# A Fourier mixing kernel: both turns of a batch in four chunks, the inverse matrices formed on the chip

## The chip, the cores and the metric

The kernel runs on one core of a Trainium2 chip. The metric is device time in microseconds. The kernel before was run three times: 861.09 us in the median, 858.69 to 861.26. Engines are named as in the profile: PE (TensorE matmuls), PEld (its weight loads), DVE (VectorE), ACT (ScalarE), POOL (GpSimd), SP (SyncE); SP, POOL and, in one place, ACT issue DMAs from their instruction queues.

## What is computed

The input x has 8 batches of 3008 tokens with 256 channels. First comes a global filter along the sequence, then a two-layer network with a leaky activation whose slope belongs to the hidden unit:

```python
X = np.fft.rfft(x, axis=1)
Y = X * (filt_r + 1j * filt_i)[None]
x = np.fft.irfft(Y, n=3008, axis=1).reshape(24064, 256)
h = x @ w_in                                    # 256 -> 2048
g = np.maximum(h, 0) + alpha * np.minimum(h, 0)
out = g @ w_out                                 # 2048 -> 256
```

Inputs and output are float32; the kernel works in float16 with float32 accumulation.

## The kernel before

**The transform.** 3008 is 47 times 64, so a token index is written as 64 times s1 plus s2, and the transform is done in two steps, forward and back. For each batch there are four kinds of pieces:

- piece_a (L162, 16 per batch): the transform over s1. The input chunk `xs` has 94 partitions (two halves of s2, each with the 47 values of s1), and each matmul with `wf1_s` gives 96 rows and 512 columns, evicted into `asb`. Input comes in four chunks of two DMAs each (load_x, L120, on POOL's queue, which turns float32 into float16).
- piece_b (L184, 12 per batch): the transform over s2 with its twiddle factors, one 128 x 128 matrix `twf_s[:, k1]` per frequency k1, two frequencies per piece. It reads `at`. DVE then multiplies the result with the filter into `uu` and with the filter's swapped halves `filts_s` into `ww`. Batch 0 uses piece_b0 (L195), which gets the swapped product from two more matmuls of 64 columns of weights, so that it need not wait for `filts_s`.
- piece_c (L211, 12 per batch): the inverse over s2, `twi_s[:, k1, 0]` times `uu` plus `twi_s[:, k1, 1]` times `ww`, evicted into `v`.
- piece_d (L238, 16 per batch): the inverse over s1 with `wi3_s`; its weights are slices of `zt`, so that its result comes transposed, channels on partitions, as the network wants it; evicted into `yT`.

**The turns.** Between piece_a and piece_b, rows and partitions change places (s1's frequency must leave the partitions, s2 must come in), and again between piece_c and piece_d. Both turns go through DRAM. On the way in, save_a (L171) writes a quarter of `asb` at a time to `a_dram[b, row, s, d]` in runs of 4 KB, and turn_a (L175) then reads the whole batch with four DMAs in runs of 512 bytes (one channel row): 3072 runs. In batch 0 it is eight half DMAs, half from SP's queue and half from ACT's. On the way back, turn_c (L224) writes a quarter of `v` with four DMAs in runs of 512 bytes, and after the last quarter reads everything in four DMAs in runs of 4 KB, each of which brings what four pieces of piece_d need. Every tile named here exists once; `a_dram` and `v_dram` have room for all batches.

**The network.** Tokens go in blocks of 512 (one of 384 per pair of batches), 48 blocks. A block has 16 steps. In step j, Block.up (L327) makes the 128 hidden rows j with two matmuls into `hps`; every second step ACT evicts two of them into `gt`, and DVE applies the slope with three instructions. In the same step Block.down (L344) does a sixteenth of the previous block's second layer, four matmuls of 256 columns; finished results go through `osb` to DRAM with stores on SP's queue (L316).

**The order of work** is written out by hand; no scheduler moves anything. Up to piece_d number 3 of batch 0 there is a prologue (L258 to L297) without network work. Then the main loop (L392) counts steps through all blocks, 768 in all, and after up and down of a step it issues the pieces that `plan` holds for that step. plan_fft (L364) puts a batch's pieces there: piece_a from step a0 every ga steps, a save after every fourth, the load of the next batch's chunk one step later, turn_a at step ta, piece_b from b0 every gap steps, piece_c three steps after its piece_b, turn_c, and piece_d from d0. Since every engine and every DMA queue works in program order, a DMA on SP that waits holds back all DMAs behind it, stores too.

Two PSUM banks (`psF`) are handed out in turn to piece_a, piece_b, piece_c and piece_d, so a piece waits until the one two before it has been read by ACT or DVE. `p_uw` holds two pairs of `uu` and `ww`, `p_x` four input chunks.

**Loads in the prologue.** SP loads `wf1_s`, the slopes, and half of `twf_s`; after turn_a the two halves of `twi_s` (L265, L267), the second half of `twf_s` and `wi3_s`. POOL loads the input of batch 0, then all eight parts of the filter (L142), and copies one column of `at` into a tile `gate` (L273), which makes its queue wait for the turn; then come `win_s` and `wout_s` (L275, L277), a copy from `zt` (L293), and the input of batch 1 (L295). `filts_s` is copied from `filt_s` on SP behind turn_c (L291).

Of the kernel before, what the change touches and what calls it, by code (L numbers as in the profile page):

```python
# [13 lines left out]
NFFT = 3008  # L14
# [11 lines left out]
def _build_consts():  # L26

    s1 = np.arange(N1)
    s2 = np.arange(N2)
    k1 = np.arange(NK1)
    p = np.arange(64)
    k2 = np.where(p < 32, p, 95 - p)
    g = np.where(p < 32, 1.0, -1.0)

    a1 = 2 * np.pi * np.outer(s1, k1) / N1
    wf1 = np.zeros((2 * N1, 96))  # L40
    wi3 = np.zeros((96, 2 * N1))
    scale = np.where(k1 == 0, 1.0, 2.0) / NFFT
    for h in range(2):
        r = slice(h * N1, h * N1 + N1)
        wf1[r, h * 48 : h * 48 + NK1] = np.cos(a1)
        wf1[r, h * 48 + NK1 : h * 48 + 48] = -np.sin(a1)
        wi3[h * 48 : h * 48 + NK1, r] = (np.cos(a1) * scale).T
        wi3[h * 48 + NK1 : h * 48 + 48, r] = (-np.sin(a1) * scale).T
# [4 lines left out]
    twf = np.empty((128, NK1, 128))  # L53
    twf[:64, :, :64], twf[64:, :, :64] = c, s
    twf[:64, :, 64:], twf[64:, :, 64:] = -s * g, c * g
    ec, es = c.transpose(2, 1, 0), s.transpose(2, 1, 0)
    gp = g[:, None, None]
    twi = np.empty((128, NK1, 2, 128))
    twi[:64, :, 0, :64], twi[:64, :, 0, 64:] = ec, es
    twi[64:, :, 0] = -twi[:64, :, 0]  # L60
    twi[:64, :, 1, :64], twi[:64, :, 1, 64:] = -es * gp, ec * gp
    twi[64:, :, 1] = twi[:64, :, 1]
    return wf1, wi3, twf, twi
# [3 lines left out]
def kernel(  # L67
# [11 lines left out]
    wf1_np, wi3_np, twf_np, twi_np = _build_consts()  # L79
# [3 lines left out]
    twi_d = nc.inline_tensor(twi_np.astype(np.float16), name="c_twi")  # L83
# [12 lines left out]
    a_dram = dram.tile([NB, 96, NH, D], FP16, name="a_dram")  # L96
    v_dram = dram.tile([NB, 96, NH, D], FP16, name="v_dram")
# [6 lines left out]
    twi_s = konst.tile([128, NK1, 2, 128], FP16, name="twi_s")  # L104
    filt_s = konst.tile([128, NK1, D], FP16, name="filt_s")
# [32 lines left out]
    xc = {(0, c): load_x(0, c) for c in range(4)}  # L138
    nc.sync.dma_start(out=al16, in_=moe_alpha.rearrange("(j p) -> j p", p=128))
    nc.sync.dma_start(out=twf_s[:, 0:12], in_=twf_d.ap()[:, 0:12])  # L140
    for ka, kb in ((0, 12), (12, 24)):
        load_filt(filt_s, 0, filt_r, ka, kb)  # L142
        load_filt(filt_s, 64, filt_i, ka, kb)
# [8 lines left out]
    class Fft:  # L152
# [18 lines left out]
        def save_a(self, c):  # L171
            s = slice(8 * c, 8 * c + 8)
            nc.sync.dma_start(out=a_dram[self.b, :, s], in_=self.asb[:, s])

        def turn_a(self, eng, ka=0, kb=NK1):  # L175
            for h in range(2):
                for c in range(2):
                    r = h * 48 + c * NK1
                    q = c * 64 + NH * h
                    eng.dma_start(  # L180
                        out=self.at[q : q + NH, ka:kb],
                        in_=a_dram[self.b, r + ka : r + kb].rearrange("k s d -> s k d"))
# [40 lines left out]

        def turn_c(self, q):  # L224
            k = 6 * q
            for h in range(2):
                for c in range(2):
                    r = h * 48 + c * NK1 + k
                    p = c * 64 + NH * h
                    nc.sync.dma_start(  # L230
                        out=v_dram[self.b, r : r + 6].rearrange("k s d -> s k d"),
                        in_=self.v[p : p + NH, k : k + 6])
            if q == 3:
                for g in range(4):
                    s = slice(8 * g, 8 * g + 8)
                    nc.sync.dma_start(out=self.zt[:, s], in_=v_dram[self.b, :, s])
# [20 lines left out]

    f0 = Fft(0)  # L258
    for i in range(16):
# [33 lines left out]
    nc.gpsimd.tensor_copy(gate[0:96, 1:2], f0.zt[:, 31, 0:1])  # L293
    for c in range(4):
# [69 lines left out]
    def plan_fft(b, a0, ga, ta, b0, gap, d0):  # L364
# [3 lines left out]
        for c in range(4):  # L368
            put(a0 + ga * (4 * c + 3), f.save_a, c)
            if b + 1 < NB:  # L370
                put(a0 + ga * (4 * c + 3) + 1,
                    lambda b=b, c=c: xc.update({(b + 1, c): load_x(b + 1, c)}))
        put(ta, f.turn_a, nc.sync)
# [61 lines left out]
```

## Time and profile before

| what | us |
|---|---|
| median of three runs | 861.09 |
| profiled execution, span from first to last instruction | 861.4 |
| PE busy | 799.4 |
| DVE busy | 612.9 |
| ACT busy | 586.6 |
| first matmul of piece_a (L168) | 7.54 |
| first matmul of piece_b0 (L200) | 33.05 |
| last matmul of piece_c of batch 0 (L221) | 53.81 |
| first matmul of piece_d (L243) | 63.08 |
| first matmul of the main loop (L332) | 64.62 |
| first matmul of piece_b of batch 1 (L188) | 110.36 |

The profiled execution spans 861.4 us, 0.3 above the median of the runs. How to read it: a line of the profile gives a line of the kernel, the engine, the operation, and output and input tile by name; "idle before" is the time in which the engine stood still just before, with what released it. PE's busy time is modelled from pipelined matmuls, so 93% does not say how near PE is to its peak; distances from start to start tell more. "PEclk" is the share of TensorE's clock that was granted; the clock fell to half after longer idle stretches of PE and came back some microseconds after work began again. The share of the DMA engines is a mean over 16. In the window 20 to 40 us that share reads 1.14, that is, all 16 were full.

### The profile page before, as it was taken

Reading aid. Unit: us, or ns where it says so; the run is one execution under the profiler, and the core shown is the slowest. Engines: PE = TensorE matmul, PEld = TensorE weight load, DVE = VectorE, ACT = ScalarE, POOL = GpSimd, SP = SyncE. Lnnn points to the kernel's source line nnn. Section 1 sums busy time; section 2 is a strip of 40 time slices with the busy share of each in tenths; the row PEclk is TensorE's granted clock in tenths of the full one; section 3 lists DMA queues with packets and bytes.
Section 4 is the critical chain, followed back from the end, with each engine's and each line's share of the span. In section 5 each row is a group of like instructions: output and inputs, shape, how many; then the busy total and the mean of one; then the engine's idle time right before and its main releaser. Section 6 shows DMA issues by size and latency. Waiting matters only on the chain.

```text
span 861.4 us, 15404 instructions
## 1 busy us (share of the span) xinstructions
PE 799.4 (93%) x5809; PEld 541.7 (63%) x5809; DVE 612.9 (71%) x1361; ACT 586.6 (68%) x817; POOL 41.4 (5%) x85
## 2 busy tenths in 40 slices
PE   3458989979999999999999999999999999999997
PEld 1134556756666766676666766676666766676665
DVE  2246668758877787678877787778877788777773
ACT  2027757767787767777777767777777866677663
POOL 4103000000000000000000000000000000000000
PEclk9989989999999999999999999999999999999999
DMA  9989835761368224772268323682148122411111
GB/s 212 250 171 197 179 69 133 157 144 41 75 148 199 60 62 97 172 158 51 53 162 195 73 64 83 164 181 50 43 120 186 50 68 50 129 38 39 39 41 49
DMA packets 95378, 95.95 MB, mean 111 GB/s; under 512 B 8312, under 2 KB 85128, under 8 KB 95176
## 3 DMA queue, kind: packets, MB, share of 16 engines
q1 hardware_dynamic: 85448, 78.19, 35.8%
q0 software_dynamic: 8256, 16.00, 12.3%
q10 hardware_dynamic: 1600, 0.79, 0.5%
q8 instruction: 45, 0.74, 0.4%
q14 instruction: 29, 0.24, 0.1%
HBM read 59.55 MB, written 49.81 MB: 127 GB/s over the span
## 4 chain that ended last, share of the span: by engine, by line
PE 70%; DVE 13%; ACT 7%; DMA 6%; issue 2%; SPq 1%; POOL 0%; ACTq 0%; DVEq 0%; POOLq 0%
PE hps L332 29%; PE op L350 28%; ACT gt L337 6%; DVE gt L341 4%; DVE m L340 4%; PE psF L168 3%; DVE ww L192 3%; DVE uu L191 3%; PE psF L221 2%; DMA at<-a_dram 2%; PE psF L243 2%; DMA a_dram<-asb 2%; PE psF L220 1%; DMA xs<-in_x_dram 1%; PE psF L188 1%
## 5 line engine op out<-in xcount | busy, mean ns | idle before, releaser
L337 ACT ACTIVATE gt<-hps 128x1024 f16<-128x1024 f32 (+1 forms) x384 | 385.1, 1003 | 134.6 <-PE hps L332 134.1
L332 PE MATMUL hps<-yT,win_s 128*128 128x512 f16 (+1 forms) x1536 | 454.3, 377 | 1.1 <-ACT yT L250 1.0
L350 PE MATMUL op<-wout_s,gt 128*128 128x256 f16 x3008 | 453.3, 273 | 0.6 <-DVE gt L341 0.6
L350 PEld LDWEIGHTS <-gt 128*128 128x128 f16 x3008 | 294.4, 98 | 192.5 <-issue 2.8
L340 DVE TENSOR_SCALAR m<-gt,alm_s 128x512 f16<-128x512 f16 (+1 forms) x768 | 233.5, 346 | 164.1 <-ACT gt L337 162.8
L341 DVE TENSOR_TENSOR gt<-gt,m 128x1024 f16<-128x1024 f16 (+1 forms) x384 | 261.6, 681 | 24.3 <-DVE m L340 0.9
L332 PEld LDWEIGHTS <-win_s 128*128 128x128 f16 x1536 | 145.6, 98 | 31.6 <-issue 5.0
L250 ACT ACTIVATE asb<-psF 96x512 f16<-96x512 f32 x120 | 70.7, 593 | 40.2 <-PE psF L168 40.2
L250 ACT ACTIVATE v<-psF 128x512 f16<-128x512 f32 x84 | 50.2, 598 | 34.9 <-PE psF L221 34.9
L250 ACT ACTIVATE yT<-psF 128x376 f16<-128x376 f32 x120 | 58.1, 484 | 20.9 <-PE psF L243 20.7
L191 DVE TENSOR_TENSOR uu<-psF,filt_s 128x512 f16<-128x512 f32 x84 | 57.4, 683 | 6.7 <-PE psF L188 6.7
L355 ACT ACTIVATE osb<-op 128x512 f32<-128x512 f32 x96 | 56.3, 587 | 6.9 <-PE op L350 3.7
L168 PE MATMUL psF<-xs,wf_s 94*96 94x512 f16 x120 | 47.8, 398 | 11.0 <-DMA xs<-in_x_dram 8.3
L192 DVE TENSOR_TENSOR ww<-psF,filts_s 128x512 f16<-128x512 f32 x84 | 57.1, 679 | 0.0
L123 POOL DMA_DIRECT2D xs<-in_x_dram x64 | 32.9, 522 | 458.2 <-PE psF L168 457.1
L243 PE MATMUL psF<-wi_s,zt 96*128 96x94 f16 x504 | 42.7, 207 | 10.8 <-DMA zt<-v_dram 9.0
L243 PEld LDWEIGHTS <-zt 96*128 96x128 f16 x512 | 36.3, 100 | 18.9 <-DMA zt<-v_dram 9.3
L221 PE MATMUL psF<-ww,twi_s 128*128 128x256 f16 x168 | 41.1, 272 | 6.2 <-DVE ww L192 3.5
L220 PE MATMUL psF<-uu,twi_s 128*128 128x256 f16 x168 | 42.9, 272 | 1.1 <-ACT yT L250 0.5
L188 PE MATMUL psF<-at,twf_s 128*128 128x256 f16 x168 | 32.3, 274 | 8.1 <-issue 4.5
L220 PEld LDWEIGHTS <-twi_s 128*128 128x128 f16 x192 | 19.0, 99 | 18.0 <-issue 13.2
L250 ACT ACTIVATE v<-op 128x512 f16<-128x512 f32 x12 | 7.2, 597 | 32.4 <-PE op L221 32.4
(35 smaller groups left out, 130.8 us busy)
## 6 DMA issues: line engine op xcount, KB each, us to landing
out_dram<-osb SPq DMA_DIRECT2D x128, 128.0 KB
a_dram<-asb SPq DMA_DIRECT2D x32, 384.0 KB
v_dram<-v SPq DMA_DIRECT2D x128, 96.0 KB
zt<-v_dram SPq DMA_DIRECT2D x32, 384.0 KB
xs<-in_x_dram POOLq DMA_DIRECT2D x64, 188.0 KB, 5.1
at<-a_dram SPq DMA_DIRECT2D x28, 384.0 KB
twi_s<-c_twi SPq DMA_DIRECT2D x2, 768.0 KB
filts_s<-filt_s SPq DMA_DIRECT2D x2, 768.0 KB
```

What stands on the lines that cost most here:

```text
L168: nc.tensor.matmul(ps[0:96], wf1_s, xs[:, o : o + 512], start=True, stop=True)
L191: nc.vector.tensor_mul(uu, px, filt_s[:, 2 * kp : 2 * kp + 2])
L192: nc.vector.tensor_mul(ww, px, filts_s[:, 2 * kp : 2 * kp + 2])
L220: nc.tensor.matmul(pv[:, kh], twi_s[:, k1, 0], uu[:, kh], start=True, stop=False)
L221: nc.tensor.matmul(pv[:, kh], twi_s[:, k1, 1], ww[:, kh], start=False, stop=True)
L243: nc.tensor.matmul(ps[:, m], self.zt[:, 8 * g + 4 * mh + m, dh * 128 : dh * 128 + 128], wi3_s, start=True, stop=True)
L250: nc.scalar.activation(o, i, AF.Copy)
L332: nc.tensor.matmul(self.hps[:, j % 2, 0:tn], win_s[:, kt, j * 128 : (j + 1) * 128], yT[:, kt, self.t0 : self.t0 + tn], start=(kt == 0), st ...
L337: nc.scalar.activation(g[:, :, 0:tn], self.hps[:, :, 0:tn], AF.Copy)
L340: nc.vector.tensor_scalar(m[:, i, 0:tn], g[:, i, 0:tn], 0.0, a, OP.min, OP.mult)
L341: nc.vector.tensor_add(g[:, :, 0:tn], g[:, :, 0:tn], m[:, :, 0:tn])
L350: nc.tensor.matmul(self.op[:, si % 2], self.gts[k][:, 128 * si : 128 * si + 128], wout_s[:, k], start=(k == 0), stop=(k == 15))
```

## The change

It has four parts.

1. **The turns run in four chunks, scattered when written and contiguous when read.** `a_dram` becomes `[batch, 4, 8, 96, 256]`: save_a of a quarter c writes 96 x 8 runs of 512 bytes, and the new turn_a(c) reads that quarter into 32 partitions of `at`, 12 KB contiguous for each. `v_dram` becomes `[batch, 4, 12, 64, 256]`: save_c(q) writes a quarter with two DMAs of 64 partitions (runs of 512 bytes as before), and turn_c(q) reads it into 24 partitions of `zt`, 16 KB contiguous each. All turns are issued by SP. Partition order in `at` and rows in `asb` and `zt` change with it, and so do the constants `wf1_s`, `wi3_s` and `twf_s`.
2. **`twi_s` is formed on TensorE.** It is no longer a constant of 1.5 MB. form_twi transposes 64 columns of `twf_s` at a time by a matmul with a permutation matrix or its negative (`perm_s`, 64 KB): eight matmuls of 128 columns, one eviction of 512 columns, for two frequencies. Six of the twelve go ahead of batch 0's piece_a, six after it. Both halves of `twf_s` are loaded at the start for that.
3. **Loads are held.** The second half of the filter is loaded behind the first gate (`at` of batch 0 has landed), with `win_s`; `wout_s` is loaded behind the second gate (`zt` has landed), ahead of batch 1's input.
4. **The plan moves.** piece_c comes four steps after its piece_b. Batch 1: turns from step 17 on, piece_b from step 34 every 4 steps (it was 40, every 3). Batch 2: turns from step 80 (it was 86). Later batches: turns from 33 steps before the reference step (it was 22). save_c comes five steps after a quarter's last piece_b, its turn four steps later.

```diff
-    twi_d = nc.inline_tensor(twi_np.astype(np.float16), name="c_twi")
+    perm_d = nc.inline_tensor(perm_np.astype(np.float16), name="c_perm")
...
-    a_dram = dram.tile([NB, 96, NH, D], FP16, name="a_dram")
-    v_dram = dram.tile([NB, 96, NH, D], FP16, name="v_dram")
+    a_dram = dram.tile([NB, 4, 8, 96, D], FP16, name="a_dram")
+    v_dram = dram.tile([NB, 4, 12, 64, D], FP16, name="v_dram")
...
     xc = {(0, c): load_x(0, c) for c in range(4)}
+    nc.sync.dma_start(out=perm_s, in_=perm_d.ap())
+    for ka in (0, 12):
+        nc.sync.dma_start(out=twf_s[:, ka : ka + 12], in_=twf_d.ap()[:, ka : ka + 12])
     nc.sync.dma_start(out=al16, in_=moe_alpha.rearrange("(j p) -> j p", p=128))
-    nc.sync.dma_start(out=twf_s[:, 0:12], in_=twf_d.ap()[:, 0:12])
-    for ka, kb in ((0, 12), (12, 24)):
-        load_filt(filt_s, 0, filt_r, ka, kb)
-        load_filt(filt_s, 64, filt_i, ka, kb)
+    load_filt(filt_s, 0, filt_r, 0, 12)
+    load_filt(filt_s, 64, filt_i, 0, 12)
...
         def save_a(self, c):
-            s = slice(8 * c, 8 * c + 8)
-            nc.sync.dma_start(out=a_dram[self.b, :, s], in_=self.asb[:, s])
-
-        def turn_a(self, eng, ka=0, kb=NK1):
-            for h in range(2):
-                for c in range(2):
-                    r = h * 48 + c * NK1
-                    q = c * 64 + NH * h
-                    eng.dma_start(
-                        out=self.at[q : q + NH, ka:kb],
-                        in_=a_dram[self.b, r + ka : r + kb].rearrange("k s d -> s k d"))
+            nc.sync.dma_start(
+                out=a_dram[self.b, c].rearrange("s r d -> r s d"),
+                in_=self.asb[:, 8 * c : 8 * c + 8])
+
+        def turn_a(self, c):
+            nc.sync.dma_start(
+                out=self.at[32 * c : 32 * c + 32],
+                in_=a_dram[self.b, c].rearrange("s (q k) d -> (s q) k d", q=4))
...
+        def save_c(self, q):
+            for c in range(2):
+                nc.sync.dma_start(
+                    out=v_dram[self.b, q, 6 * c : 6 * c + 6].rearrange("k s d -> s k d"),
+                    in_=self.v[64 * c : 64 * c + 64, 6 * q : 6 * q + 6])
+
         def turn_c(self, q):
-            k = 6 * q
...
+            nc.sync.dma_start(
+                out=self.zt[24 * q : 24 * q + 24],
+                in_=v_dram[self.b, q].rearrange("a (h s) d -> (a h) s d", h=2))
...
+    def form_twi(kp, evict):
+        ps = bank(True).rearrange("p (k t n) -> p k t n", k=2, t=2)
+        for kh in range(2):
+            for t in range(2):
+                for half in range(2):
+                    nc.tensor.matmul(
+                        ps[64 * half : 64 * half + 64, kh, t],
+                        twf_s[:, 2 * kp + kh, 64 * t : 64 * t + 64],
+                        perm_s[:, 1 if (t, half) == (0, 1) else 0],
+                        start=True, stop=True)
+        evict(twi_s[:, 2 * kp : 2 * kp + 2], ps)
+
     f0 = Fft(0)
+    for kp in range(6):
+        form_twi(kp, both[kp % 2])
     for i in range(16):
         f0.piece_a(i, both[i % 2], i % 2 == 1)
         if i % 4 == 3:
             f0.save_a(i // 4)
-    f0.turn_a(nc.sync, 0, 12)
-    f0.turn_a(nc.scalar, 12, 24)
-    nc.sync.dma_start(out=twi_s[:, 0:12], in_=twi_d.ap()[:, 0:12])
-    nc.sync.dma_start(out=twf_s[:, 12:24], in_=twf_d.ap()[:, 12:24])
-    nc.sync.dma_start(out=twi_s[:, 12:24], in_=twi_d.ap()[:, 12:24])
+        if i >= 7 and i % 4 == 3:
+            f0.turn_a(i // 4 - 1)
+    f0.turn_a(3)
+    for kp in range(6, 12):
+        form_twi(kp, both[kp % 2])
...
     nc.gpsimd.tensor_copy(gate[:, 0:1], f0.at[:, 11, 0:1])
+    load_filt(filt_s, 0, filt_r, 12, 24)
+    load_filt(filt_s, 64, filt_i, 12, 24)
     for kt in range(2):
         nc.gpsimd.dma_start(out=win_s[:, kt], in_=moe_w_in[kt * 128 : (kt + 1) * 128])
-    for q in range(2):
-        nc.gpsimd.dma_start(
-            out=wout_s[:, 8 * q : 8 * q + 8],
-            in_=moe_w_out[1024 * q : 1024 * q + 1024].rearrange("(j p) d -> p j d", p=128))
...
         if kp >= 3 and kp % 3 == 0:
+            f0.save_c(kp // 3 - 1)
             f0.turn_c(kp // 3 - 1)
     f0.piece_c(11, on_act, psO.tile([128, 2, D], FP32, name="op"))
+    f0.save_c(3)
     f0.turn_c(3)
...
     nc.gpsimd.tensor_copy(gate[0:96, 1:2], f0.zt[:, 31, 0:1])
+    for q in range(2):
+        nc.gpsimd.dma_start(
+            out=wout_s[:, 8 * q : 8 * q + 8],
+            in_=moe_w_out[1024 * q : 1024 * q + 1024].rearrange("(j p) d -> p j d", p=128))
...
         for c in range(4):
-            put(a0 + ga * (4 * c + 3), f.save_a, c)
+            save = a0 + ga * (4 * c + 3)
+            put(save, f.save_a, c)
+            put(max(save + 4, ta + c), f.turn_a, c)
...
-        put(ta, f.turn_a, nc.sync)
         for kp in range(12):
             put(b0 + gap * kp, f.piece_b, kp)
-            put(b0 + gap * kp + 3, f.piece_c, kp, on_act)
+            put(b0 + gap * kp + 4, f.piece_c, kp, on_act)
         for q in range(4):
-            put(b0 + gap * (3 * q + 2) + 4, f.turn_c, q)
+            save = b0 + gap * (3 * q + 2) + 5
+            put(save, f.save_c, q)
+            put(save + 4, f.turn_c, q)
...
-    plan_fft(1, 10, 1, 26, 40, 3, 92)
-    plan_fft(2, 50, 2, 86, 104, 5, 187)
+    plan_fft(1, 10, 1, 10, 34, 4, 92)
+    plan_fft(2, 50, 2, 80, 104, 5, 187)
     for b in range(3, NB):
         p = 96 * (b - 1)
-        plan_fft(b, p - 54, 2, p - 22, p + 6, 5, p + 91)
+        plan_fft(b, p - 54, 2, p - 33, p + 6, 5, p + 91)
```

More of the change, by code (lines that the diff above doesn't have):

```diff
@@ L39, in _build_consts @@
     a1 = 2 * np.pi * np.outer(s1, k1) / N1
-    wf1 = np.zeros((2 * N1, 96))
-    wi3 = np.zeros((96, 2 * N1))
-    scale = np.where(k1 == 0, 1.0, 2.0) / NFFT
+    wf1 = np.zeros((2 * N1, 2, 2, NK1))
+    wi3 = np.zeros((4, 2, 6, 2, 2 * N1))
+    scale = np.where(k1 == 0, 1.0, 2.0)[:, None] / NFFT
     for h in range(2):
         r = slice(h * N1, h * N1 + N1)
[L45 to L48, printed above, removed]
+        wf1[r, 0, h] = np.cos(a1)
+        wf1[r, 1, h] = -np.sin(a1)
+        wi3[:, 0, :, h, r] = (np.cos(a1).T * scale).reshape(4, 6, N1)
+        wi3[:, 1, :, h, r] = (-np.sin(a1).T * scale).reshape(4, 6, N1)
     kk = k1[:, None] + 47 * k2[None, :]
@@ L52, in _build_consts @@
     c, s = np.cos(ang), np.sin(ang)
[L53 to L63, printed above, removed]
+    twf = np.empty((2, 64, NK1, 128))
+    twf[0, :, :, :64], twf[1, :, :, :64] = c, s
+    twf[0, :, :, 64:], twf[1, :, :, 64:] = -s * g, c * g
+    cc, s8, ri, h = np.unravel_index(np.arange(128), (4, 8, 2, 2))
+    row = 64 * ri + NH * h + 8 * cc + s8
+    twf = twf.reshape(128, NK1, 128)[row]
+    perm = np.zeros((128, 2, 128))
+    perm[np.arange(128), 0, row] = 1.0
+    perm[np.arange(128), 1, row] = -1.0
+    return wf1.reshape(2 * N1, 96), wi3.reshape(96, 2 * N1), twf, perm
 @with_exitstack
@@ L78 @@
     nc = tc.nc
-    wf1_np, wi3_np, twf_np, twi_np = _build_consts()
+    wf1_np, wi3_np, twf_np, perm_np = _build_consts()
     wf1_d = nc.inline_tensor(wf1_np.astype(np.float16), name="c_wf1")
@@ L104 @@
     twi_s = konst.tile([128, NK1, 2, 128], FP16, name="twi_s")
+    perm_s = konst.tile([128, 2, 128], FP16, name="perm_s")
     filt_s = konst.tile([128, NK1, D], FP16, name="filt_s")
@@ L222, in piece_c @@
             evict(self.v[:, 2 * kp : 2 * kp + 2], pv)
-        def turn_c(self, q):
-            k = 6 * q
[L226 to L236, printed above, removed]
+        def save_c(self, q):
[3 more added lines that the diff above has]
+                    in_=self.v[64 * c : 64 * c + 64, 6 * q : 6 * q + 6])
+        def turn_c(self, q):
+            nc.sync.dma_start(
+                out=self.zt[24 * q : 24 * q + 24],
+                in_=v_dram[self.b, q].rearrange("a (h s) d -> (a h) s d", h=2))
         def piece_d(self, i, evict, wide=False):
@@ L368, in plan_fft @@
         for c in range(4):
-            put(a0 + ga * (4 * c + 3), f.save_a, c)
+            save = a0 + ga * (4 * c + 3)
+            put(save, f.save_a, c)
+            put(max(save + 4, ta + c), f.turn_a, c)
             if b + 1 < NB:
-                put(a0 + ga * (4 * c + 3) + 1,
+                put(save + 1,
                     lambda b=b, c=c: xc.update({(b + 1, c): load_x(b + 1, c)}))
-        put(ta, f.turn_a, nc.sync)
         for kp in range(12):
             put(b0 + gap * kp, f.piece_b, kp)
-            put(b0 + gap * kp + 3, f.piece_c, kp, on_act)
+            put(b0 + gap * kp + 4, f.piece_c, kp, on_act)
         for q in range(4):
-            put(b0 + gap * (3 * q + 2) + 4, f.turn_c, q)
+            save = b0 + gap * (3 * q + 2) + 5
+            put(save, f.save_c, q)
+            put(save + 4, f.turn_c, q)
         for i in range(16):
```

## The prediction

> **What bounds the kernel now.** I read the slices and the page's shares first, then the list of waits, the chain of work that ended last in order of time, and last the timeline of single stretches.
>
> ```profile
> span 861.4 us, 15404 instructions
> PE 799.4 (93%) x5809; PEld 541.7 (63%) x5809; DVE 612.9 (71%) x1361; ACT 586.6 (68%) x817; POOL 41.4 (5%) x85
> PE   3458989979999999999999999999999999999997
> ...
> PEclk9989989999999999999999999999999999999999
> DMA  9989835761368224772268323682148122411111
> ```
>
> PE is full from the tenth slice (200 us) on. All sizeable PE idling lies before, and the DMA engines are nearly full exactly there. The waits (total, times, longest):
>
> ```profile
> PE psF L200 <- DMA at<-a_dram: 17.9, 1, 17.9
> PE psF L243 <- DMA zt<-v_dram: 9.0, 1, 9.0
> PE psF L188 <- issue: 4.5, 1, 4.5
> PE psF L188 <- DMA at<-a_dram: 3.6, 1, 3.6
> PE psF L221 <- DVE ww L192: 3.5, 12, 0.3
> PE psF L168 <- ACT v L250: 2.0, 5, 0.5
> ```
>
> The first two belong to batch 0, before the main loop; the next two to batches 1 and 2 (at 105.9 and 182.9 us), both waiting for `at`. The chain shows what each was (start, length):
>
> ```profile
> 15.74 6.18 DMA a_dram<-asb
> 23.40 9.52 DMA at<-a_dram
> ...
> 56.08 2.00 DMA v_dram<-v
> 58.20 4.83 DMA zt<-v_dram
> ...
> 69.41 7.13 DMA xs<-in_x_dram
> ...
> 168.02 7.56 DMA a_dram<-asb
> ```
>
> In the full part one small wait repeats: the second matmul of piece_c waits for `ww` (timeline: start, length):
>
> ```profile
> 304.59 0.68 DVE L192 TENSOR_TENSOR ww<-psF,filts_s 128x512 f16<-128x512 f32 x1
> ...
> 304.91 0.27 PE L220 MATMUL psF<-uu,twi_s 128*128 128x256 f16 x1
> ...
> 305.33 0.27 PE L221 MATMUL psF<-ww,twi_s 128*128 128x256 f16 x1
> ```
>
> These start 0.42 us apart; undisturbed pairs start 0.109 apart. From 200 us on, 32 pairs are late, 11.5 us together.
>
> **The change, part by part.** T is a time in the profile; minus is a gain.
>
> *1. Batch 0 up to `at` (PE restarts at 33.05).* Six form_twi go ahead of piece_a. The trace has no such group; the nearest row is the pair of 64-wide matmuls of L203, 256 columns in 0.34 us at the low clock, so 0.17 for 128 columns, four pairs 0.7 us, 4.2 us for six. The lower end is the alternating eviction (16 piece_a in 6.9 us, 0.43 each): 2.6 us; the upper 6 us, if the halves run one after the other. I take 4.2: the last `asb` is ready near 19 instead of 15.7. The DMA engines decide: by the packet records, up to 33 us they carried (16 engines together) xs 7.6 us, filters 9.6, half of twf 1.0, saves 384 packets of 4 KB at 170 ns = 4.1, turns 3072 of 512 B at 45 ns = 8.6: 30.9 us. After: xs 7.6, half the filters 4.8, twf and perm 2.2, saves 3072 of 512 B at 28 to 44 ns (the `v` saves) = 5.4 to 8.4, turns 128 of 12 KB at 470 ns (twice the 234 of a 6 KB twi packet) = 3.7: 23.7 to 26.7 us. With the 2.1 us that 33 stands over its own load, and some 2.8 for the last save and turn, each awaited (a `v` save lands in 1.9 us of which 0.4 is data), 28.6 to 31.6. SP now holds save 2 behind turn 0's wait and save 3 behind turn 1's; followed by hand this also gives 29.5, which I take (27 to 32): -3.5. The last six form_twi lie under this wait. The turns that ACT's queue issued (1.9 us, ACT idle) go to SP, which waits anyway; al16 comes later, and is not used before the forms: nothing. The clock: PE idles 15 to 33 us now and is at half speed to 44.05; it would idle some 6 us after the forms, and after 54.08 the clock halved within 3.6 us, so I leave the loop's 20.8 us as they are.
>
> [...]
>
> *2. The turn back of batch 0.* From the first save (54.74) to `zt` were 8.3 us: four issues and their landing 3.3, read 4.83. Two saves of 64 partitions take one issue interval each off: 2.7. The read's quarter is now 24 rows of 16 KB contiguous; there is no such row. Lower end 2.5 us (25 GB/s per engine, as xs and twf packets), upper 5 (13 GB/s, as the 4 KB packets of `zt` at 300 ns). I take 3.0, since twi's long contiguous rows are nearest: -2.4, `zt` at 57.1.
>
> [...]
>
> *3. Loads gone and held.* The two twi_s loads (256 packets of 6 KB, 4 us of DMA at 32 to 38 us) delayed no matmul, the first L220 (35.74) coming 0.8 us after the first half landed: their going is worth nothing by itself, and makes room for the held loads. filt's second half and win_s go behind `at`: 4.8 and 5.2 us of DMA under the 20.8 us loop, needed at its middle and end: nothing, and if the filters were 3 us late, that. wout_s goes behind `zt` and ahead of xs(1) in POOL's queue. By the packets: filts_s 128 at 0.9 us = 7.2 us from 56.5 on, wout_s 2048 at 60 ns = 7.7, first xs chunk 1.9: it lands near 73.8. PE asks for it 12.9 us after the first piece_d (63.08 to 75.96 now), at 70. So a wait of 3.8 instead of 0.71, at the edge of losing the clock. Of the 5.9 us of steps 1 and 2 this leaves 2.9; with a part of a cold start (5.4 us at half speed cost 2.7 after 110.36) I book -2.0 (-5 to +0.5).
>
> *4. `at` of batch 1* (stall 4.48 plus 2.7 of half clock = 7.2). Turn chunks now start from step 17, but piece_b is wanted at step 34, not 40, 5 steps after the last turn. Saves under xs traffic landed 5.1 to 6.1 us after issue; four steps take 4.3; and turn c waits on SP ahead of save c+1, so the lag adds up. Save 3 is ready 17.3 us after the first piece_a, issued near 20.4, lands near 24, turn 3 near 26.4; wanted at 23.7. Stall 2.7 (0, were saves as quick as unhindered `v` saves; 6 plus cold at most). With part of a cold start: -3.5 (-7.2 to +1.5).
>
> *5. piece_c, piece_b, piece_a in one step.* In batch 1 (gap 4, offset 4) this happens at steps 50, 54 ... 78, eight times; before, the 0.47 us wait `psF` L168 on `v` came four times there. +1.8 (0 to +2.5).
>
> *6. `zt` of batch 1, a new wait.* piece_d stays at step 92, but the last save_c moves to step 83 and turn_c to 87, and on SP between them stands turn 3 of batch 2, waiting for its save 3 (issued at 80, some 5 us), then three stores of 2.2 us, then turn_c behind 1.5 MB of turns. I get `zt` 15 us after step 80; piece_d comes after 9.8. Stall 5, some 1.7 of cold clock, less a 1.0 us wait that stood at 174.3: +6 (+1 to +9).
>
> *7. `at` of batch 2* is asked for at step 104, 20 steps after the last turn (18 before, and `zt`'s burst of 1.5 MB no longer sits in front): the stall of 3.6 and its 3.4 us at half clock go: -5.3 (-3 if a rest stays).
>
> *8. piece_c one step later.* A step is 0.87 us, `ww` is late by 0.26 to 0.48. But where a piece_a falls two steps before, it takes over px's bank and waits instead (three of five per batch while the next batch's piece_a run). What stays gone is 4.8 us in batches 2 to 6 and 2.2 in batch 7; the moved ones cost 0.11 more, 1.6: -5.4 (-11.5 to -4).
>
> Everything else, save and turn per batch from batch 3 on, has 20 steps of cover; if a turn stuck on SP for over those 17 us, piece_b would stall.
>
> Sum: -2.0 - 3.5 + 1.8 + 6 - 5.3 - 5.4 = -8.4. The profiled execution, 861.4, stands at the median (861.09): 853. The bounds add to 833 and 868.
>
> **Rivals.**
> - *SP's queue decides (slower).* Turn c's wait ahead of save c+1 makes each save as late as the sum of all before. For it: 7.56 us for a save at 168.02. Against: unhindered `v` saves of 1.9 us. Steps 4 and 6 at their bad ends (+1.5, +9), the rest as booked: -2.0+1.5+1.8+9-5.3-5.4 = -0.4, and one lost clock at the first xs (2.7), `at` of batch 0 at 32 (2.5): 866. It decides when a save takes over some 6.5 us.
> - *The waits simply go.* The chunked reads are as short as their bytes and nothing is late on SP: step 4 -7.2, step 6 +1, others booked: -17.1, and 1.5 more with `at` at 28: 843. For it: 512 B packets at 28 ns.
> - *No visible change.* The held wout_s gives back batch 0's gain (0) and step 6 takes all of step 4: 0+0+1.8+6-5.3-5.4 = -2.9, with `ww` waits that only move (+2): 860. For it: xs(1) already ended a wait at 76.67.
>
> **How the numbers follow.** The forecast case has 0.50 (847 to 858), the slower rival 0.20, the waits going 0.18, no change 0.12. 0.3% (2.6 us) is about what can be told from no change: faster 0.68, same 0.12, slower 0.20. The range 841 to 866 leaves out the far ends of both outer rivals.
>
> **What would show it.** Right: L188 never waits near 180 us; PE's first piece_b near 29 to 30; a wait for xs of 2 to 5 us near 70; a wait of piece_d for `zt` near 165 to 175; fewer late L221. Wrong: saves of 512 B packets landing in over 7 us, a stall of piece_b from batch 3 on, or the clock lost more than three times after 60 us.

## The result, and the profile after

The changed kernel takes 869.44 us in the median (868.66 to 871.72), beside 860.71 for the kernel before on the same chip: a ratio of 1.0106, 95% interval 1.0088 to 1.0124. It is about 1.1% slower. I had forecast 853.0 (841 to 866), 0.9% faster, so sign and range were both wrong. The profiled execution spans 867.7 us, 6.3 more than the one before.

The page of the changed kernel, shares and slices (40 slices of 21.7 us):

```profile
span 867.7 us, 15539 instructions
...
PE 802.8 (93%) x5905; PEld 549.0 (63%) x5905; DVE 618.6 (71%) x1367; ACT 591.3 (68%) x823; POOL 41.6 (5%) x85
...
PE   5547969969999999999999999999999999999997
...
PEclk9977979979999999999999999999999999999999
DMA  9869825661369233771458224761347123311111
```

The busy shares are the same as before; only the first slices tell. PE now has gaps in slices 1 to 4, 6 and 9, and the clock is down in four of the first nine slices. Behind them both kernels look alike at this resolution. The waits of PE say which they are (total, times, longest):

```profile
PE psF L239 <- DMA zt<-v_dram: 23.9, 2, 15.3
PE psF L199 <- DMA at<-a_dram: 8.7, 1, 8.7
PE psF L187 <- DMA at<-a_dram: 8.4, 1, 8.4
...
PE psF L170 <- ACT v L246: 4.6, 13, 0.5
PE psF L170 <- DMA xs<-in_x_dram: 1.5, 1, 1.5
```

The waits for turns were 17.9 and 9.0 us in batch 0, 4.5 and 3.6 later. They are now 8.7 (`at`, batch 0, behind six form_twi), 15.3 (`zt`, batch 0), 8.4 (`at`, batch 1) and 8.6 (`zt`, batch 1, new). No wait of piece_c for `ww` is left in the steady part: a second matmul of piece_c follows the first like this everywhere (timeline of the changed kernel: start, length):

```profile
304.77 0.27 PE L219 MATMUL psF<-uu,twi_s 128*128 128x256 f16 x1
304.88 0.27 PE L220 MATMUL psF<-ww,twi_s 128*128 128x256 f16 x1
304.99 0.27 PE L219 MATMUL psF<-uu,twi_s 128*128 128x256 f16 x1
305.10 0.27 PE L220 MATMUL psF<-ww,twi_s 128*128 128x256 f16 x1
```

All starts are 0.11 us apart. Before, 32 pairs were late by 11.5 us together; after, none.

The best single view is the start of each step of the main loop in both traces (first matmul of Block.up of that step, in us):

| start of step | before | after | difference | what lies since the line above | booked in the prediction |
|---|---|---|---|---|---|
| 16 | 81.8 | 88.0 | +6.2 | prologue, `xs` of batch 1 | -2.0 (steps 1 to 3) |
| 50 | 123.0 | 133.1 | +10.1 | `at` of batch 1: +3.9 | -3.5 (step 4) |
| 92 | 170.2 | 182.5 | +12.3 | three pieces in one step: +2.2 | +1.8 (step 5) |
| 96 | 173.9 | 196.8 | +22.8 | `zt` of batch 1: +10.5 | +6 (step 6) |
| 110 | 193.2 | 210.6 | +17.4 | `at` of batch 2: -5.4 | -5.3 (step 7) |
| 767 | 847.8 | 854.3 | +6.5 | the steady part: -10.9 | -5.4 (step 8) |

Step 0 itself, which stands in no row, begins at 69.4 us instead of 64.6: +4.7, where steps 1 and 2 of the prediction had -5.9; the wait for `xs` and the clock lost with it add the rest of the first row.

So the change is two things: a steady part that gains twice what I had booked, and a start that has lost 22.8 us by step 96, of which batch 2 gives back 5.4. Two rows fit their booking (steps 5 and 7). The other three of the start are off by 8.2, 7.4 and 4.5 us, the steady part by 5.5 the other way; together that is, within 0.2, the 14.7 us by which the profiled span missed the forecast.

How the turns are late is read from the chain of work that ended last, in order of time (start, length; the changed kernel):

```profile
52.28 4.52 DMA v_dram<-v
57.21 0.57 SPq L225
57.84 4.55 DMA v_dram<-v
62.40 5.35 DMA zt<-v_dram
...
94.79 5.34 DMA a_dram<-asb
100.50 6.14 DMA a_dram<-asb
107.01 4.43 DMA a_dram<-asb
111.45 3.80 DMA at<-a_dram
...
181.12 5.96 DMA v_dram<-v
187.14 4.79 DMA zt<-v_dram
```

Before, the chain went through one save and one read per turn. Now several saves stand one behind the other, though they carry different quarters and nothing in the data orders them. SP's queue orders them. Its timeline in batch 1 (when an instruction left the queue, and how long it took to issue):

```profile
87.74 0.33 SPq L174 DMA_DIRECT2D a_dram<-asb  x1
94.37 0.31 SPq L179 DMA_DIRECT2D at<-a_dram  x1
94.79 0.53 SPq L174 DMA_DIRECT2D a_dram<-asb  x1
100.15 0.30 SPq L179 DMA_DIRECT2D at<-a_dram  x1
100.50 0.42 SPq L174 DMA_DIRECT2D a_dram<-asb  x1
101.02 1.46 SPq L330 DMA_DIRECT2D out_dram<-osb  x2
106.66 0.31 SPq L179 DMA_DIRECT2D at<-a_dram  x1
107.01 0.42 SPq L174 DMA_DIRECT2D a_dram<-asb  x1
111.45 0.30 SPq L179 DMA_DIRECT2D at<-a_dram  x1
```

Each turn_a (L179) leaves when its own save has landed, 4.4 to 6.6 us after that was issued, and the next save (L174) leaves only then. The quarters of `asb` are ready every four steps, 4.3 us apart, and the queue takes them 5.7 to 7 us apart. By the last quarter, ready near 99.5, the queue is 7.5 us behind. In all, SP stood 75.9 us in 19 waits of turn_a and 31.1 us in 16 of turn_c.

My theory at this point: the loss is SP's order (a turn's wait in front of the next save) plus reads that are dearer than I had booked; the gain is the one step that piece_c moved, and nothing else. The experiments take these apart. Their "before" was run beside them each time (861.2 to 862.2 us).

### The profile page after: what moved, and what is told of

The parts are those of the page before. It is cut to its first block, busy times and chain, and to the rows that moved or that the text cites. A ratio compares the mean times of both kernels' runs of the same rounds, so it can differ in the third digit from the quotient of the medians.

```text
span 867.7 us, 15539 instructions
## 1 busy us (share of the span) xinstructions
PE 802.8 (93%) x5905; PEld 549.0 (63%) x5905; DVE 618.6 (71%) x1367; ACT 591.3 (68%) x823; POOL 41.6 (5%) x85
## 4 chain that ended last, share of the span: by engine, by line
PE 86%; DMA 8%; ACT 3%; issue 1%; DVE 0%; SPq 0%; POOL 0%; ACTq 0%; POOLq 0%; DVEq 0%
PE op L364 36%; PE hps L346 35%; PE psF L170 3%; DMA a_dram<-asb 3%; PE psF L239 2%; PE psF L220 2%; PE psF L187 2%; PE psF L219 2%; DMA v_dram<-v 2%; DMA xs<-in_x_dram 1%; DMA zt<-v_dram 1%; ACT v L246 1%; DMA at<-a_dram 1%; PE hps L202 1%; ACT gt L351 1%
## 5 line engine op out<-in xcount | busy, mean ns | idle before, releaser
L351 ACT ACTIVATE gt<-hps 128x1024 f16<-128x1024 f32 (+1 forms) x384 | 385.1, 1003 | 133.1 <-PE hps L346 128.2
L239 PE MATMUL psF<-wi_s,zt 96*128 96x94 f16 x504 | 43.0, 209 | 25.5 <-DMA zt<-v_dram 23.9
L239 PEld LDWEIGHTS <-zt 96*128 96x128 f16 x512 | 36.8, 101 | 33.7 <-issue 30.0
L187 PEld LDWEIGHTS <-twf_s 128*128 128x128 f16 x168 | 15.7, 98 | 11.3 <-DMA at<-a_dram 8.7
```

Source lines behind the costliest of these rows:

```text
L187: nc.tensor.matmul(px[:, kh], twf_s[:, k1], self.at[:, k1], start=True, stop=True)
L239: nc.tensor.matmul(ps[:, m], self.zt[:, 8 * g + 4 * mh + m, dh * 128 : dh * 128 + 128], wi3_s, start=True, stop=True)
L351: nc.scalar.activation(g[:, :, 0:tn], self.hps[:, :, 0:tn], AF.Copy)
```

## The experiments

### 1. piece_c one step later, alone

The kernel before, with that one offset:

```diff
-            put(b0 + gap * kp + 3, f.piece_c, kp, on_act)
+            put(b0 + gap * kp + 4, f.piece_c, kp, on_act)
...
-            put(b0 + gap * (3 * q + 2) + 4, f.turn_c, q)
+            put(b0 + gap * (3 * q + 2) + 5, f.turn_c, q)
```

> The kernel before with one number changed: piece_c four steps after its piece_b instead of three (turn_c one step later with it). Theory A (the late second matmul of piece_c is waiting for ww and a step of 0.87 us covers it wholly): the 32 late pairs after 200 us vanish, 11.5 us and the 1.5 us of waits ahead of L220 with them, so 848 to 852 us. Rival (the wait only moves to the piece that takes over px's PSUM bank, as the prediction's step 8 had it): 855 to 857 us, and new waits of 0.3 to 0.5 us at L168 or L243.

Measured: 852.79 us, ratio 0.9889 (0.9853 to 0.9925). Step by step it is at +1.9 after the wait for `xs` (which was 2.8 us in this run and cost the clock for 3.4 us), at -0.3 at step 110 and at -11.2 at the last step. The steady part gains 10.9 us, the same as in the changed kernel. The median is 0.8 us above the range that I had given, less than the 1.9 that `xs` cost here. The rival, that these waits only move onto piece_a, falls: no second matmul of piece_c is late, and piece_a waits in the steady part five times for 0.17 us.

### 2. The same step taken back in the changed kernel

```diff
-            put(b0 + gap * kp + 4, f.piece_c, kp, on_act)
+            put(b0 + gap * kp + 3, f.piece_c, kp, on_act)
```

> The changed kernel with piece_c three steps after its piece_b, as before the change; saves and turns stay where the change put them. Theory A (the steady part's gain of 11 us comes from that one step and from nothing else in the change): ww is late again in batches 2 to 7, 30 or more late second matmuls of piece_c with 10 to 12 us, and 878 to 882 us. Rival (the gain comes in part from the turns' new form or place, less traffic on SP or fewer DMA runs beside the work): 870 to 876 us.

Measured: 877.60 us, ratio to the kernel before 1.0178 (1.0159 to 1.0197). The wait is back in PE's list:

```profile
PE psF L220 <- DVE ww L191: 3.7, 13, 0.3
```

Again 32 second matmuls start late, by 11.47 us together (11.46 in the kernel before). From step 105 on this kernel loses 10.9 us against the changed one; between steps 16 and 105 it gains 3.9, where three pieces of batch 1 no longer meet in one step, and so the median came out 0.4 us below the range that I had given. With experiment 1 this closes the point from both sides: the turns' new form has no part in the steady gain.

### 3. The turns' order on SP: batch 0

turn_c of a quarter is issued behind the save of the next quarter, not ahead of it:

```diff
             f0.save_c(kp // 3 - 1)
-            f0.turn_c(kp // 3 - 1)
+            if kp >= 6:
+                f0.turn_c(kp // 3 - 2)
     f0.piece_c(11, on_act, psO.tile([128, 2, D], FP32, name="op"))
     f0.save_c(3)
+    f0.turn_c(2)
     f0.turn_c(3)
```

> The changed kernel; in batch 0 alone each turn_c is issued one quarter later, behind the next quarter's save_c. Theory A (SP's order): save 3 leaves at 54 instead of 57.2 us, zt is complete near 64 instead of 67.7: 864 to 867 us. Rival (the reads of 24 rows of 16 KB are slow themselves, 2.7 us of data each, and two of them now stand together at the end): zt at 67 or later, 868 to 870.

Measured: 863.66 us, ratio 1.0027 (1.0009 to 1.0045), 5.8 us less than the changed kernel and a little better than I expected. The last two links of batch 0 in its chain:

```profile
52.96 3.81 DMA v_dram<-v
56.84 4.81 DMA zt<-v_dram
```

In the changed kernel the last quarter of `v` was evicted at 53.19 and its save left SP at 57.21, 4.0 us later, behind turn_c(2)'s wait. Here it was evicted at 52.31 and left at 52.34. Step 0 starts at 63.3 instead of 69.4. What stays is a save of 4.4 us and a read of 4.8, 9.2 together, where the old turn took 8.3.

### 4. The turns' order on SP: batch 1

turn_a one step later, so that the next save is ahead of it:

```diff
-            put(max(save + 4, ta + c), f.turn_a, c)
+            put(max(save + 5, ta + c), f.turn_a, c)
```

> The changed kernel, turn_a five steps after its save instead of four, so that on SP save c+1 stands ahead of turn c. Only batch 1's order moves. Theory A (each turn that waits on SP for its save holds back the next save, and the lag adds up over four chunks): save 3 leaves near 100 us instead of 107.0, at lands near 109 instead of 115.3, the wait of L187 falls from 8.4 us to 1 to 3 and the cold clock after it with it: 860 to 864 us. Rival (the reads and writes themselves are slow under the input's traffic, the order does not matter): save 3 may leave earlier but lands as late, wait still over 6 us, 867 to 870.

Measured: 865.21 us, ratio 1.0045 (1.0027 to 1.0063), 4.2 less than the changed kernel. The last save left at 99.41, when its data were ready (107.01 in the changed kernel), but it then took 7.1 us to land among the input of batch 2, and the read 4.2. The wait for `at` fell from 8.45 to 4.75 us. So 7.6 us of queue bought 3.7 us of waiting: save and read took 3.1 us longer, as the rival had it, and PE asked 0.8 us earlier. The result lies between the two theories.

### 5. zt of batch 1

piece_b every three steps, as before the change, so that the last turn_c no longer falls among batch 2's turns:

```diff
-    plan_fft(1, 10, 1, 10, 34, 4, 92)
+    plan_fft(1, 10, 1, 10, 34, 3, 92)
```

> The changed kernel, batch 1's piece_b every 3 steps instead of 4, from the same step 34. Theory A (step 92's wait of 8.6 us comes from the plan: save_c of the last quarter at step 83 and its turn at 87 behind batch 2's turns): now at steps 72 and 76, the wait goes wholly, with the cold clock after it: 10 to 11 us less by step 96; the eight triples of piece_c, piece_b and piece_a go too, 1 to 2 us: 856 to 860 us. Rival (the DMA engines are full there, the read of zt is late wherever it is issued): a wait of more than 4 us stays at step 92, 865 to 869.

Measured: 857.54 us, ratio 0.9946 (0.9925 to 0.9966). PE waits for `zt` only once now, in batch 0:

```profile
PE psF L239 <- DMA zt<-v_dram: 17.9, 1, 17.9
```

The 8.6 us wait at step 92 and the 3.6 us of work at half clock behind it are gone; the difference to the kernel before stays at +13.0 from step 84 to 104, where it had jumped to 22.8. This one number was worth 11.9 us, more than the change as a whole had lost.

### 6. What the reads cost by themselves

A kernel that only reads 393 KB (a quarter of a turn) from DRAM again and again, one read at a time:

```python
def read(p0, n, st, f, o=0):      # n rows of f elements into partitions p0, p0 + st, ...
    nc.sync.dma_start(
        out=dst[p0 : p0 + (n - 1) * st + 1 : st, 0:f],
        in_=scr[o : o + n * f].rearrange("(p f) -> p f", p=n))
```

> This kernel leaves the whole transform and the network out: its output is zeros, and it reads a quarter of a turn (393 KB) from DRAM into SBUF in many forms, one read at a time, nothing else running, with a read of 128 rows of 3 KB between any two. In the changed kernel 24 rows of 16 KB cost 1.0 to 1.1 us per packet and 4.3 us from issue to landing, 32 rows of 12 KB 0.78 to 0.84 us per packet and 3.8 to 4.1 us; I had booked 0.65 and 0.47 us, 3.0 and 2.4 us. Theory A (the rows' neighbourhood: all rows of a read lie in one stretch of 24 or 32 partitions, and writing there is slower than 25 GB/s per engine): the same 24 rows spread over every fourth partition take 0.65 us per packet, 32 spread rows 0.47, and 128 or 96 rows over all partitions are as fast; the compact ones stay at 1.0 and 0.8 here too. Rival B (the length of the row: a packet over 4 KB or so goes at 15 GB/s wherever it lies): spread and compact rows cost the same 1.0 and 0.8 us, and 96 rows of 16 KB cost 1.0 as well, while 128 rows of 3 KB go at 0.12 to 0.15 us each. Rival C (the reads of the kernel were slow only because the saves' small packets and the input ran beside them, or the bytes had just been written): every form here goes at 25 GB/s per engine, 24 rows of 16 KB land 3.0 us after issue, 32 of 12 KB 2.4.

Measured, at least two readings each, from the packet records and from issue to the last signal of landing (the last row but one reads four quarters at once):

| read of 393 KB | mean packet, ns | first packet's start to last one's end, us | issue to landing, us |
|---|---|---|---|
| 128 rows of 3 KB, all partitions | 142 to 179 | 1.5 to 1.9 | 2.8 to 3.2 |
| 96 rows of 4 KB, partitions 0 to 95 | 196, 213 | 1.6, 1.9 | 3.2, 3.5 |
| 64 rows of 6 KB, partitions 0 to 63 | 371, 387 | 2.0, 2.0 | 4.0, 4.0 |
| 32 rows of 12 KB, neighbouring partitions | 743 to 800 | 1.9 to 2.1 | 3.7 to 3.8 |
| 32 rows of 12 KB, every fourth partition | 591, 646 | 1.5, 1.7 | 3.1, 3.3 |
| 24 rows of 16 KB, neighbouring partitions | 1007 to 1152 | 2.4 to 2.9 | 4.2 to 4.7 |
| 24 rows of 16 KB, every fourth partition | 893, 942 | 2.2, 2.6 | 4.5, 4.7 |
| 16 rows of 24 KB, partitions 0 to 15 | 2402, 2428 | 3.1, 3.1 | 5.1, 5.2 |
| 96 rows of 16 KB, partitions 0 to 95 (1573 KB) | 1091, 1098 | 7.3, 7.4 | 8.8, 8.8 |
| 768 runs of 512 B into 32 partitions | 29, 31 | 2.0, 2.4 | 3.8, 4.1 |

Rival C falls at once: alone on the chip the two forms of the kernel cost 3.7 to 3.8 and 4.2 to 4.7 us, about what they cost in the changed kernel (3.8 and 4.8 to 5.35 for the last reads of a turn). Between A and B the answer is mixed. The 32 rows of 12 KB are quicker when spread, by 0.4 us of data time and 0.6 us in all, and then nearly as quick as 128 rows; so the neighbourhood is a real part. But spread packets still take 0.6 us, not the 0.47 that A asked for, and the 24 rows of 16 KB gain hardly anything by being spread (0.2 to 0.3 us of data, given back by the longer issue: 0.8 instead of 0.3 us). I can't say from these runs what holds those at 0.9 us. B's own test, 96 rows of 16 KB spread over all of partitions 0 to 95, gave 1.1 us per packet, as B asked. But that read moved 215 GB/s in all, and 96 rows of 4 KB over the same partitions 203 to 240, so long rows alone did not make a read slower there. The last row is the one that matters for the change: runs of 512 bytes into the same 32 partitions land at most 0.4 us later than contiguous rows of 12 KB (3.8 and 4.1 us beside 3.7 to 3.8). For a quarter read by itself, contiguity gained next to nothing.

In the changed kernel's trace a read of 24 rows (`zt`, issued at 62.40) has 12 signals of landing and one of 32 rows (`at`, issued at 111.45) has 16. That this makes the 24 rows slower no run here shows: in every fourth partition they still took 4.5 to 4.7 us. Nor do the readings go by the number of partitions alone: 64 rows of 6 KB took 4.0 us, 32 neighbouring rows of 12 KB 3.7 to 3.8.

### 7. The plan alone, without the new turns

The kernel before with its own turns and constants, and only steps moved:

```diff
-            put(b0 + gap * kp + 3, f.piece_c, kp, on_act)
+            put(b0 + gap * kp + 4, f.piece_c, kp, on_act)
...
-    plan_fft(1, 10, 1, 26, 40, 3, 92)
-    plan_fft(2, 50, 2, 86, 104, 5, 187)
+    for half in range(2):
+        put(9 + half, copy_filts, half)
+    plan_fft(1, 10, 1, 26, 43, 3, 92)
+    plan_fft(2, 50, 2, 82, 104, 5, 187)
```

> The kernel before, with its own turns, constants and loads, and only its plan moved: piece_c four steps after its piece_b (as in the first experiment, 852.8 us), piece_b of batch 1 from step 43 instead of 40, the turn of batch 2 at step 82 instead of 86, filts_s copied at steps 9 and 10 instead of behind turn_c of batch 0. Theory A (the turns in chunks bring nothing that moved steps would not): of the 852.8, the wait for xs and its lost clock go (-1.9), the wait for at of batch 1 falls from 4.8 to some 2.2 us and keeps the clock (-2.6 and -2), the wait for at of batch 2 goes (-2.6): 842 to 846 us, as good as the combined kernel (844.6). Rival (the chunks matter: a whole turn starts only when the last save has landed, and then moves 1.5 MB): at of batch 1 or 2 stays late by 4 us or more, or zt of batch 1 becomes late at step 92, and it stays at 849 to 853 us.

Measured: 850.12 us, ratio 0.9859 (0.9840 to 0.9878). By its time the rival won, but only one of its reasons did. The wait for `at` of batch 1 came out at 2.19 us and that of batch 2 went, as A had it, though behind the first the clock stood at half speed for 3.4 us. What A had not seen is a new wait of 3.5 us for `zt` of batch 1 at step 92: the whole read starts when the last of 16 saves has landed (169.69), and takes 3.8 us. And the wait for `xs` did not go (1.8 us and the clock again), so the copy of filts_s was not its cause. The three waits that are left, 7.5 us and three stretches of lost clock, were not corrected in a further plan; so this run does not show how far the old turns can be brought by their plan alone.

### 8. The change with its plan corrected

Experiments 3, 4 and 5 together in the changed kernel, and three more edits: piece_b of batch 1 from step 39, two of batch 1's input chunks ahead of `wout_s`, filts_s copied in the main loop.

```diff
-    for q in range(2):
+    for c in range(2):
+        xc[(1, c)] = load_x(1, c)
+    for q in range(2):
         nc.gpsimd.dma_start(
             out=wout_s[:, 8 * q : 8 * q + 8],
...
-            put(max(save + 4, ta + c), f.turn_a, c)
+            put(max(save + 5, ta + c), f.turn_a, c)
...
-    plan_fft(1, 10, 1, 10, 34, 4, 92)
+    for half in range(2):
+        put(9 + half, copy_filts, half)
+    plan_fft(1, 10, 1, 10, 39, 3, 92)
```

> The changed kernel with the three corrections of the runs before together (turn_a of later batches one step later, turn_c of batch 0 a quarter later, batch 1 with three steps between piece_b), and three more: piece_b of batch 1 from step 39 instead of 34, so that it asks for at when that has landed; batch 1's first two input chunks ahead of wout_s on POOL's queue; filts_s copied at steps 9 and 10 instead of behind turn_c of batch 0. Theory A (what the change loses is lost in these places alone, and the steady part keeps its 11 us): step 0 near 63, no wait for xs, at of batch 1 late by 0 to 1 us, no wait for zt of batch 1, no lost clock after step 0: against the kernel before -1.4 at step 0, -1 for xs and the clock, -5 to -7 for at of batch 1, +1.5 for banks in batch 1, -5.3 at batch 2, -11 steady: 838 to 844 us. Rival (the reads of 4 us and SP's order keep PE waiting somewhere else, wherever the request is moved): a new wait of 4 us or more before step 110, and 847 to 853 us, no better than the kernel before with piece_c one step later (852.8).

Measured: 844.62 us, ratio 0.9791 (0.9741 to 0.9841), just above theory A's range and outside the rival's. PE's list of waits has one line too many for A:

```profile
PE psF L239 <- DMA zt<-v_dram: 11.1, 1, 11.1
PE psF L199 <- DMA at<-a_dram: 8.9, 1, 8.9
...
PE psF L239 <- issue: 3.4, 1, 3.4
```

`xs` is not waited for any more, `at` of batch 1 for 0.4 us, and the clock stays up from 68.8 to 167.8 us. But 3.4 us at L239 are again `zt` of batch 1 at step 92 (a wait for several semaphores, put down to "issue"). The read left SP at 159.55, behind one read of `at` for batch 2 and ahead of three more, and its last signal of landing came 8.6 us later, at 168.17.

### 9. The turns of batch 2 behind that read

```diff
-    plan_fft(2, 50, 2, 80, 104, 5, 187)
+    plan_fft(2, 50, 2, 84, 104, 5, 187)
```

> The combined kernel (844.6 us) with one number changed: the turns of batch 2 from step 84 instead of 80, so that SP issues the last turn_c of batch 1 (step 81) ahead of them and not among them. There the last read of zt took 8.0 us from issue to landing (159.55 to 167.59) among three reads of at, PE waited 3.35 us for it at step 92 and lost the clock for 3.4 us. Theory A (the read is late because other reads stand beside it on the DMA engines): it lands 4.4 to 5 us after its issue, near 164.3, the wait of piece_d falls to under 1 us, the clock is kept, at of batch 2 still comes 10 us before it is asked for, and the kernel takes 839 to 841 us. Rival (SP's own stores and the save's landing hold it back whatever stands behind): it lands at 166 or later, the wait stays over 2 us, 843 to 846 us.

Measured: 840.69 us, ratio 0.9745 (0.9728 to 0.9762), the time that A asked for. SP's timeline, L230 being the read of `zt`, L179 those of `at`:

```profile
160.19 0.52 SPq L174 DMA_DIRECT2D a_dram<-asb  x1
160.81 0.68 SPq L230 DMA_DIRECT2D zt<-v_dram  x1
161.59 2.23 SPq L179 DMA_DIRECT2D at<-a_dram  x3
```

It is now ahead of all reads of `at` but close to three of them, and landed 6.9 us after its issue, at 167.72: not the 4.4 to 5 us that A named, and as late as the rival had it (166 or later). The wait is 1.1 us, between the two, and the clock is kept to the end. The 3.9 us gained are the shorter wait (2.2) and the stretch of 3.4 us at half clock that did not come (some 1.7). That the other reads beside it are the cause is not shown: in experiment 10, with the same order, the read took 7.9 us and the wait was 2.1, so the order shortened the read by 0.7 to 1.7 us. (The 8.0 us in the text above is 8.6 by the last signal.)

### 10. Every fourth partition in the kernel

A quarter of `at` into every fourth partition, with the rows of `twf_s` in the matching order:

```diff
-    cc, s8, ri, h = np.unravel_index(np.arange(128), (4, 8, 2, 2))
+    s8, ri, h, cc = np.unravel_index(np.arange(128), (8, 2, 2, 4))
...
-                out=self.at[32 * c : 32 * c + 32],
+                out=self.at[c : c + 125 : 4],
```

> The last kernel (840.7 us) with one layout changed: a quarter of at is read into every fourth partition instead of 32 neighbouring ones; the order of the rows of twf_s and of the permutation follows. The 32 rows of 12 KB stay as they are. Alone on the chip the spread read landed 3.1 to 3.3 us after its issue, the compact one 3.7 to 3.8 (that is the price measured without other traffic). Theory A (the neighbourhood of the partitions costs this in the kernel too): the last two reads of at in batch 0 take 3.2 to 3.4 us instead of 3.9, a packet 0.6 us instead of 0.8, PE restarts some 0.6 us earlier, and the time falls by about 0.5 us, which this measurement can't tell from nothing: 839.5 to 841. Rival (beside other traffic the reads go at the pace of the traffic): 3.8 us or more per read, and no change, or a loss of up to 1 us from the longer issue (0.48 instead of 0.32 us).

Measured: 840.88 us, ratio 0.9759 (0.9738 to 0.9780), the same as experiment 9, as both theories allow. The read's own time decides. The last one of batch 0 in the chain:

```profile
27.36 3.27 DMA at<-a_dram
```

It was 3.86 us in experiment 9 and 3.83 in the changed kernel, and the one before it fell from 3.86 to 3.26. A holds for the read. Its 0.6 us in batch 0 is too small to be seen in the whole.

## Why the prediction was wrong, step by step

- **Step 1 (`at` of batch 0 at 29.5): right in kind, 2.2 us short.** It landed at 31.65. The six form_twi ahead of piece_a took 4.3 us (7.29 to 11.62; booked 4.2), and the last `asb` was ready at 19.4 (booked 19). The last save then left SP 1.8 us late and took 6.6 us, and the read 3.8 us, 1.4 more than the 2.4 that step 4 has for such a read.
- **Step 2 (`zt` of batch 0): this one failed first.** I booked the last quarter alone, save and read, 5.9 us after its data. It took 14.6: 4.0 us on SP behind turn_c(2), 5.2 for the save, 5.35 for the read. This is the largest single miss, 8.7 us. I had named this mechanism in step 4 and not looked for it here, where the quarters come 5 us apart and each save takes that long. Experiment 3 cuts the 14.6 to 9.3 by order alone. The read's price was wrong too: both ends of my range, 2.5 and 5 us, came from rows in other places (`twi` rows over 128 partitions, 4 KB rows over 96). I took 3.0, by the nearest row in length; the upper end would have been nearer, since the read took 5.35 us here and 4.2 to 4.7 alone on the chip.
- **Step 3 (held loads): half right.** A wait for `xs` came, 1.5 us instead of 3.8, and with it a lost clock (83.1 to 86.5). In experiment 8, with two chunks ahead of `wout_s` and step 0 earlier, it was gone; these two edits were not tried apart.
- **Step 4 (`at` of batch 1): the lag was named and sized too small.** The last save left 24.9 us after the first piece_a, not 20.4, since each link of the queue took 5.7 to 7 us, against quarters that are ready every 4.3. It landed 4.4 us later (booked 3.6) and the read took 3.8 (booked 2.4). PE asked 1.1 us later than I had it. 2.7 + 4.5 + 0.8 + 1.4 - 1.1 = 8.3; the trace has 8.45. Of these 8.45 us the earlier request, step 34 for 40, is some 5 (six steps of 0.87): experiment 8, which asks at step 39 and has the order of experiment 4, waits 0.4.
- **Step 5: right** (+2.2 for +1.8; the wait `psF` on `v` came 8 times at 0.47 us).
- **Step 6 (`zt` of batch 1): mechanism right, size short.** It landed 19.2 us after step 80, not 15. The wait was 8.6 us instead of 5, the work at half clock behind it 3.6 us, some 1.8 of cost, as booked, and the 1.0 us wait that I had taken off stayed (at 197.2 now): +10.5 for +6, past its upper bound of 9. Experiment 5 removes it with one number.
- **Step 7: right** (-5.4 for -5.3).
- **Step 8: mechanism right, size wrong by half.** I believed that three of five waits in batches 2 to 6 would move onto piece_a. Five waits of 0.17 us there are all that came, 0.9 us together: -10.9, near the lower end of the range (-11.5). Experiments 1 and 2 show the same 10.9 from both sides.
- **The rivals.** "SP's queue decides" (866, 0.20) was the case that came in sign, and in place for steps 4 and 6; the largest loss, `zt` of batch 0, it had not either. That its 866 lies near 869.4 is in part luck: what it booked as lost came out 7 us larger and the gain of step 8 5.5 us larger. Its condition was too strict: I had it decide above 6.5 us for a save, and saves of 4.4 to 6.6 did it, because several of them add up. "The waits simply go" and "no visible change" did not come; but with its plan corrected the kernel takes 840.7, below the 843 of the former.
- **The signs.** Two signs of being right came: no wait of piece_b near 180 us, and no late second matmul. Two came elsewhere: a wait for `xs` of 1.5 us at 82, and one of piece_d for `zt` until 192 us. The first piece_b came at 31.7 us, not at 29 to 30. The signs of being wrong did not mark the loss: the clock was lost three times after 60 us, not more, no piece_b waited from batch 3 on, and the saves that took over 7 us (five of `asb`, 7.65 to 8.5, and six of `v`, 7.16 to 8.16) came from 260 us on, where they cost nothing.
- **The clock.** From the end of a wait to the full clock the changed kernel took 10.4, 5.0, 4.4, 5.3 and 3.6 us, the kernel before 11.0, 4.9, 5.4 and 4.3. In both traces every stretch between two changes of the clock lasts a multiple of 3.41 us (at half clock 3.41, 6.83, 10.24 and 17.07). All these values but the first of each kernel are one stretch of 3.41 us and 0.2 to 2.0 us ahead of it. Why batch 0 took 10.4 and 11.0, no run here shows.

## What to carry to other kernels

When a transfer is cut into pieces so that it can start earlier, write down the issuing queue's order with each piece's landing time: a wait for piece c in front of the save of piece c+1 makes the pieces serial, and one place later in the order they are parallel again (batch 0's last save left SP 4.0 us after its data in the changed kernel, 0.03 us after them in experiment 3). Price a read by a measured one with the same rows in the same partitions, not only by the length of its rows: here 32 contiguous rows of 12 KB landed in 3.7 to 3.8 us in neighbouring partitions and in 3.1 to 3.3 in every fourth one, and the former at most 0.4 us sooner than runs of 512 bytes into the same partitions. And undo a change in parts before judging it: the same turns lost 1.1% as they were planned and won 2.5% with other step numbers and a changed order of some DMAs, while moved steps alone, with the old turns, won 1.4% in the one plan that was tried. What the turns in chunks are worth beside a plan as well tuned is not shown; ahead of the main loop they won nothing, since step 0 began at 62.7 to 66.2 us in the four kernels with turn_c in the better order and at 63.1 to 64.6 in the three with the old turns.

## What the runs showed of the hardware

- A read of 393 KB from DRAM, alone on the chip, took 2.8 to 3.2 us over all 128 partitions, 3.7 to 3.8 us into 32 neighbouring ones, 4.0 into 64 neighbouring ones and 5.1 to 5.2 into 16. Of that, 0.9 to 1.3 us passed between issue and the first packet.
- 32 rows in every fourth partition landed in 3.1 to 3.3 us; the issue itself was longer (0.48 for 0.32 us), and in the kernel the read fell from 3.86 to 3.27 us.
- Packets of 16 KB took 0.9 to 1.15 us in the mean of a read alone on the chip, 14 to 18 GB/s for one engine, and 0.9 to 1.4 us in the mean of a read of `zt` in the changed kernel; packets of 3 KB in a read over 128 partitions took 0.14 to 0.18 us, 17 to 22 GB/s. The quickest single ones in the changed kernel took 0.61 and 0.12 us, 27 and 25 GB/s.
- Saves of a quarter of `asb` in 768 runs of 512 bytes were cheap per packet in the changed kernel (27 to 33 ns in the mean, 1.3 to 1.6 us for 16 engines) and still landed 4.2 to 8.5 us after their issue, so their landing, not their bytes, set the chain.
